# Key and query stacks of an attention unit loaded in pieces of 96, 12, 48 and 6 partitions instead of 54

## The chip, the core and the metric

The kernel runs on one core of a Trainium2 chip. The time is the device time of one execution in microseconds (us); the kernel before has a median of 1902.3 us over three runs (1902.12, 1902.3, 1907.2). A core has engines that run their own instruction streams: TensorE (PE; its weight loads are shown as PEld), VectorE (DVE), ScalarE (ACT), GpSimd (POOL) and SyncE (SP). SP does no arithmetic here: it issues DMAs, in order, and waits in its queue for what a DMA needs. 16 DMA engines move the data.

## What is computed

One layer on x (2048 tokens, width 576): an adaptive layer norm whose shifts and gates come from silu(c) @ w_mod, attention with a memory over four segments of 512 tokens (32 heads of width 18), then a second adaptive layer norm and a SwiGLU feed-forward of width 4608. All in float32.

```python
for s in range(N):                       # N = 4 segments of L = 512 tokens
    logits = einsum("bhqd,bhkd->bhqk", qs, ks) * scale + mask
    p = softmax(logits)
    a_dot = einsum("bhqk,bhkd->bhqd", p, vs)
    num = einsum("bhld,bhde->bhle", phi(qs), M)
    den = einsum("bhld,bhd->bhl", phi(qs), z)[..., None] + 1e-6
    outs.append(g * (num / den) + (1 - g) * a_dot)
    M, z = M + einsum("bhld,bhle->bhde", phi(ks), vs), z + phi(ks).sum(2)
x = x + ga * (concat(outs) @ wo)
h = layernorm(x) * (1 + cb) + sb
return x + gb * ((silu(h @ w_gate) * (h @ w_up)) @ w_down)
```

## The kernel before

Float32 products are made from parts of fewer bits: a tile is split into a high part and a low part (`fh`, `fl`; `hh`, `hl`), and TensorE multiplies the parts that matter. For the attention logits this is done by stacking: a head has 18 features, and its stack has 3 × 18 = 54 rows, the high part of a key or query beside the low part of the other.

The program has four stages.

The projections (to about 256 us). For each segment `proj` (L456) makes nine tiles of keys and queries, copies each out of PSUM on ScalarE (L466), splits it (GpSimd L80, VectorE L81), and stores the parts to DRAM tensors `kD[s]` and `qD[s]` of shape (576, 3, 512): one feature, three parts, 512 tokens, so that the 54 rows of a head lie together (L471 to L478); later segments' queries are stored once more, whole, as `qF` (L480). `vproj` makes the values in eight groups a segment (copied out at L498) and `mem` (L447) the memory. `trans_in` normalizes and transposes the next segment's input (PE L236, evacuated by ScalarE at L243). The order of instructions in this stage is made by an automatic scheduler, which also places the first three stack loads and part of the first units' work: the generator `early` (L255) loads the stacks of units 0 and 1 and later of unit 2.

The loop over units (256 to 616 us). A unit is four heads of one segment, so there are 32; there the order is written out by hand (a manual schedule, with a table `PAT` of events for each of eleven steps of a unit). A unit's work is spread over three passes of the loop. First its stack is loaded by `load_stack` (L160). Then `p1_step` (L174) multiplies queries by keys (PE L184) only to get each query's largest logit on VectorE (`mx`, L189). GpSimd turns it into a high and a low part of its negative (`mc`, L194 to L197), TensorE transposes them (`pmt`, L203), ScalarE copies them (`mr`, L207), and `put_m` (L169) stores them by two small DMAs (L172) into rows 108 and 109 of the query stack. So the second product (PE L599, 110 rows) subtracts the largest logit by itself, and ScalarE's exponential (`Pt`, L606) needs no bias. Last come GpSimd's mask (L610) and the product with the values (PE `av`, L623). Other events of the loop prepare the output weights (`woraw`, loaded at L908), the output projection (`pw`, L733), its residual sum (`xr`, `xD`, L738 and L740), queries for the memory (`qf`, L776), values (`vq`, L668) and the layer norm's output (L938, L958).

The stack tiles are in SBUF: `kst` has 128 partitions x 2 x 512 floats and `qst` 128 x 4 x 512. Four buffers of each rotate (`NB = 4`). A unit's four heads are two pairs; pair a uses slot a of `kst`, and in the pair the head e has its 54 rows on partitions 54e to 54e + 53. A query's rows go to slot e + 2a and the rest of that slot is zero, so that one product over 108 rows gives one head.

SP issues all of these loads in order. Completion of its DMAs is counted on eight semaphores that are used in turn, so each DMA also waits for the one eight before it in this queue.

Behind the loop come a tail of the output projection (616 to 660 us) and the feed-forward (660 us to the end), which loads no stacks.

Of the kernel before, what the change touches and what calls it, by code (L numbers as in the profile page):

```python
# [68 lines left out]
def f32(ap):  # L69
    return ap.bitcast(F32)  # L70
# [3 lines left out]
def block(ctx: ExitStack, tc: tile.TileContext, x, wqk, wv, wo, beta, wgu, wd, c, w_mod, out):  # L74
    nc = tc.nc
# [43 lines left out]
    qst, kst = {}, {}  # L119
# [20 lines left out]
    qD = [dr.tile([D, 3, L], F32, tag=f"qD{s}", name=f"qD{s}") for s in range(NSEG)]  # L140
    kD = [dr.tile([D, 3, L], F32, tag=f"kD{s}", name=f"kD{s}") for s in range(NSEG)]
# [17 lines left out]

    def load_stack(u, b):  # L160
        s, q = units[u]
        for e in range(2):
            v = [d[s].rearrange("f z t -> (f z) t").rearrange("(Q a e r) t -> Q e r a t", Q=8, a=2, e=2)[q, e]
                 for d in (kD, qD)]
            r = slice(54 * e, 54 * e + 54)
            nc.sync.dma_start(f32(kst[b][r]), v[0])
            nc.sync.dma_start(f32(qst[b][r, e:4:2, :]), v[1])

    def put_m(u, b):  # L169
        mr = mrow.pop(u)  # L170
# [75 lines left out]
    with ExitStack() as p1:  # L246
# [8 lines left out]
        def early():  # L255
            for u in range(2):
                load_stack(u, u)
            for u in range(NE):
                yield from p1_unit(u, u, ps, "m", 1, pb, 2)
            load_stack(2, 2)  # L260
# [64 lines left out]
        with ExitStack() as p0:  # L325
# [27 lines left out]
            for p in (1, 0):  # L353
                for k in range(6):
                    for h in range(2):
                        r = 64 * (1 - p) + 32 * h
# [6 lines left out]
            for p in (1, 0):  # L363
                r = 64 * (1 - p) + 32
# [93 lines left out]
        def proj(s, t):  # L458
            hh, hl, hr = hT[s]
            pp = ps.tile([P, L], F32, tag="p", name="pp", bufs=3)  # L460
            mm14(pp, lambda k: wqkh[:, t, k, :], lambda k: wqkl[:, t, k, :], lambda k: hh[k],
                 lambda k: hl[k], lambda: hr, True)
            f = pb.tile([P, L], F32, tag="pf", name="pf")
            fh = pb.tile([P, L], F32R, tag="fh", name="fh")
            fl = pb.tile([P, L], F32R, tag="fl", name="fl")
            nc.scalar.copy(f, pp)  # L466
            split(fh, fl, f)
            k0, k1 = 128 * t, min(128 * t + 128, D)
            if k0 < D:
                n = k1 - k0  # L470
                nc.sync.dma_start(kD[s][k0:k1, 0:2, :], f32(fh[:n]).unsqueeze(1).to_broadcast([n, 2, L]))  # L471
                nc.sync.dma_start(kD[s][k0:k1, 2, :], f32(fl[:n]))
            q0, q1 = max(128 * t - D, 0), 128 * t + 128 - D
            if q1 > 0:
                n = q1 - q0
                r = P - n
                nc.sync.dma_start(qD[s][q0:q1, 0:3:2, :], f32(fh[r:]).unsqueeze(1).to_broadcast([n, 2, L]))
                nc.sync.dma_start(qD[s][q0:q1, 1, :], f32(fl[r:]))  # L478
                if s > 0:
                    nc.sync.dma_start(qF[s][q0:q1, :], f[r:])  # L480
            return f
# [34 lines left out]
        for s in range(NSEG):  # L516
# [12 lines left out]
            for t in QKORD:  # L529
# [4 lines left out]
                f = proj(s, t)  # L534
# [44 lines left out]
    def load_unit(u):  # L579
        if u < NU:  # L580
            load_stack(u, u % NB)
# [733 lines left out]
    def plain(t, p, c):  # L1315
        b, h, c = c // 4, c // 2 % 2, c % 2
        pd = ps.tile([P, 2, L], F32, tag="dn", name="pd", bufs=2)
        for i in range(2):
            tk = slice(128 * (2 * c + i), 128 * (2 * c + i) + 128)
            k = 0  # L1320
            for f in range(2):
                ah, al = AP[p % 2, (f, b)]
                dh, dl = DP[p % 2, (f, h)]
                for a, w in ((ah, dh), (ah, dl), (al, dh)):
                    nc.tensor.matmul(pd[:, i, :288], lhsT=a[:, tk], rhs=w, start=(k == 0), stop=(k == 5))  # L1325
                    k += 1
        d = x11[1] if t and b and h else acc[2 + h + 2 * b]
        o = d[:, 2 * c:2 * c + 2]
        nc.vector.tensor_tensor(o, o, pd[:, :, :288], op=ALU.add)  # L1329
        if p == NPR - 1:  # L1330
            if t:
                store(t, b, h, d, c)
            elif c == 1:
                return lambda: store(t, b, h, d)
# [9 lines left out]
    with tc.manual_schedule():  # L1344
# [6 lines left out]
        for u in range(NU + 1):  # L1351
            s, q = divmod(u, 8)
# [101 lines left out]
        for t in range(2):  # L1454
            for p in range(NPR):
# [16 lines left out]
                for k in range(14):  # L1472
                    z, m = ZM[k]
# [67 lines left out]
                    if prev is not None and is_plain(*prev):  # L1541
# [3 lines left out]
                        if CH0[t][k]:  # L1545
                            f = plain(*prev, chunk)
# [97 lines left out]
```

## Time and profile before

| | us |
|---|---|
| median of three runs | 1902.3 |
| the profiled execution: its own time | 1904.4 |
| its span, first to last instruction | 1902.7 |
| PE busy | 1851.9 (97%) |
| DVE busy | 1500.7 (79%) |
| ACT busy | 935.8 (49%) |
| POOL busy | 583.2 (31%) |
| stack loads: first issue to last | 72.6 to 570.8 |
| granted TensorE clock, mean over the span | 0.995 |

A row of the timeline has the start, the length, the engine, the line of the kernel and the operation with output and input tiles; in brackets stands how long the engine was idle before it and what ended that idle time. A row of waits says for whom an engine waited, how long in all, how often, and the longest. A row of a windows view gives, for a stretch of time, its length, each engine's busy time with the number of instructions, the granted clock of TensorE (1.00 is full speed), the mean busy share of the 16 DMA engines and GB/s. DMA issues on SP take SP's time; the transfer itself runs later on the DMA engines.

### The profile page before, as it was taken

To read this page: it belongs to the slowest core of one execution; us is meant where nothing else is said; L and a number is where in the kernel's file an instruction comes from. 1 tells how busy PE (TensorE), PEld (TensorE's weight loads), DVE (VectorE), ACT (ScalarE), POOL (GpSimd) and SP (SyncE) were. 2 spreads that over 40 slices of the span, in tenths; PEclk is the share of its full clock that TensorE was granted. 3 is DMA by queue.
4 is the path that set the end of the run, shared out by engine and by line. 5 is a ranking of instruction groups with operands and counts; after the bars stand their busy time and mean duration, and the time that the engine had idled before them with its cause. 6 is when DMAs were issued, how large, how long until landed. Compare 5 with 4: busy or idle time off the path is not lost.

```text
span 1902.7 us, 30767 instructions
## 1 busy us (share of the span) xinstructions
PE 1851.9 (97%) x10927; PEld 1573.5 (83%) x10927; DVE 1500.7 (79%) x3277; ACT 935.8 (49%) x2060; POOL 583.2 (31%) x789
## 2 busy tenths in 40 slices
PE   7999989999999899999999999999999999999999
PEld 4888866777776788888888888888888888888888
DVE  6566357878886688898897988876888888888887
ACT  1222267767777444445455454444544454454542
POOL 5212235555556544545444535400000000000000
PEclk9999999999999899999999999999999999999999
DMA  6767555445754764454454554478333233333331
GB/s 197 257 223 250 200 184 149 122 143 160 200 167 126 274 209 160 157 194 156 156 191 154 166 178 140 138 259 260 102 121 104 82 119 102 124 102 100 108 107 60
DMA packets 179425, 304.32 MB, mean 160 GB/s; under 512 B 26152, under 2 KB 107688, under 8 KB 177352
## 3 DMA queue, kind: packets, MB, share of 16 engines
q1 hardware_dynamic: 150696, 245.29, 41.0%
q10 hardware_dynamic: 28576, 57.07, 8.5%
q8 instruction: 86, 1.41, 0.3%
q14 instruction: 67, 0.55, 0.1%
HBM read 187.98 MB, written 113.77 MB: 159 GB/s over the span
## 4 chain that ended last, share of the span: by engine, by line
PE 85%; DMA 4%; DVE 3%; ACT 3%; POOL 2%; issue 1%; SPq 1%; ACTq 0%; DVEq 0%; POOLq 0%
PE A L1204 23%; PE pd L1325 13%; PE C L1204 12%; PE pd L1308 9%; PE B L1204 6%; PE pp L100 5%; PE av L623 3%; PE pv L100 3%; PE s L599 3%; PE s L184 3%; PE pw L733 1%; ACT Pt L606 1%; DMA qs<-mr 1%; PE pm L450 1%; PE pr L358 1%
## 5 line engine op out<-in xcount | busy, mean ns | idle before, releaser
L1204 PE MATMUL A<-y,wh 128*128 128x512 f32 x1152 | 404.7, 392 | 1.8 <-ACT B L1250 1.0
L189 DVE CUSTOM_DVE_ANT_0 junk<-s,tri 128x256 bf16<-128x256 f32 (+3 forms) x512 | 222.9, 485 | 76.0 <-PE s L184 57.6
L1169 DVE TENSOR_TENSOR wl<-O,wh 128x256 fp32r<-128x256 f32 x504 | 262.3, 525 | 3.5 <-ACT wh L1168 3.1
L1204 PEld LDWEIGHTS A<-y,wh 128*128 128x128 f32 x1152 | 216.7, 188 | 43.4 <-ACT B L1250 2.4
L1204 PE MATMUL A<-y,wl 128*128 128x512 f32 x576 | 224.8, 390 | 0.0
L606 ACT ACTIVATE Pt<-s 128x512 f32<-128x512 f32 (+1 forms) x352 | 188.0, 559 | 58.8 <-PE av L623 25.4
L1159 POOL TENSOR_TENSOR O<-O 128x384 f32<-128x384 f32 x140 | 157.9, 1140 | 163.3 <-DMA O<-in_wgu_dram 81.6
L1204 PE MATMUL C<-y,wh 128*128 128x512 f32 x576 | 203.7, 394 | 4.1 <-DMA y<-yD 2.9
L1313 DVE TENSOR_TENSOR acc<-acc,pd 128x576 f32<-128x576 f32 x216 | 162.3, 751 | 54.9 <-PE pd L1308 50.1
L1168 ACT CAST wh<-O 128x256 fp32r<-128x256 f32 x504 | 197.0, 405 | 3.0 <-DVE wr L1154 1.6
L1325 PE MATMUL pd<-dh,ah 128*128 128x288 f32 x640 | 189.8, 297 | 0.1
L1325 PE MATMUL pd<-dh,al 128*128 128x288 f32 x640 | 188.2, 294 | 0.0
L1325 PE MATMUL pd<-dl,ah 128*128 128x288 f32 x640 | 188.2, 294 | 0.0
L1329 DVE TENSOR_TENSOR acc<-acc,pd 128x576 f32<-128x576 f32 x156 | 116.7, 749 | 80.3 <-PE pd L1325 79.9
L599 PE MATMUL s<-qs,ks 110*128 110x512 f32 (+2 forms) x384 | 149.6, 405 | 14.0 <-ACT Pt L606 9.5
L1268 ACT CAST ah<-sg 128x512 fp32r<-128x512 f32 x192 | 119.3, 621 | 86.1 <-DVE sg L1228 80.6
L184 PE MATMUL s<-ks,qs 108*128 108x256 f32 (+3 forms) x512 | 142.2, 330 | 1.4 <-DVE mx L189 1.3
L1269 DVE TENSOR_TENSOR al<-sg,ah 128x512 fp32r<-128x512 f32 x192 | 134.6, 701 | 8.0 <-ACT ah L1268 7.7
L1308 PE MATMUL pd<-dh,ah 128*128 128x288 f32 x448 | 132.9, 297 | 0.0
L1308 PE MATMUL pd<-dl,ah 128*128 128x288 f32 x448 | 131.9, 294 | 0.0
L1308 PE MATMUL pd<-dh,al 128*128 128x288 f32 x448 | 131.2, 293 | 0.0
L1204 PEld LDWEIGHTS C<-y,wh 128*128 128x128 f32 x576 | 108.2, 188 | 24.4 <-DMA y<-yD 3.3
(364 smaller groups left out, 4408.1 us busy)
## 6 DMA issues: line engine op xcount, KB each, us to landing
O<-in_wgu_dram SPq DMA_DIRECT2D x36, 768.0 KB
oD<-O ACTq DMA_DIRECT2D x36, 512.0 KB
O<-oD SPq DMA_DIRECT2D x36, 512.0 KB
ks<-kD SPq DMA_DIRECT2D x64, 216.0 KB
qs<-qD SPq DMA_DIRECT2D x64, 216.0 KB
O<-in_wgu_dram SPq DMA_DIRECT2D x36, 384.0 KB
rD<-wr ACTq DMA_DIRECT2D x36, 336.0 KB
wr<-rD SPq DMA_DIRECT2D x35, 336.0 KB
```

The lines of the kernel that those rows point to most:

```text
L100: nc.tensor.matmul(ps, lhsT=a, rhs=b, start=(k == 0), stop=(k == 13))
L184: nc.tensor.matmul(bank[:, n * (h - h0):n * (h - h0) + n], lhsT=qst[b][0:108, h, 128 * i:128 * i + 128], rhs=kst[b][0:108, h // 2, 0:n], s ...
L189: nc.vector.tensor_tensor_reduce(junk[:, :n], bank[:, n * (h - h0):n * (h - h0) + n], tri[:, L - n:], 1.0, -3e38, op0=ALU.add, op1=ALU.max ...
L599: nc.tensor.matmul(bank[:, n * (g - h):n * (g - h + w)].rearrange("p (a b) -> p a b", a=w), lhsT=kst[u % NB][0:110, g // 2, 128 * j:128 * ...
L606: nc.scalar.activation(pt[:, h:h + per, :n], bank[:, :n * per].rearrange("p (a b) -> p a b", a=per), AF.Exp, scale=SCALE)
L1159: eng.tensor_tensor(o[:, d], o[:, a], o[:, b], op=op)
L1168: nc.scalar.copy(wh, o)
L1169: later.append(lambda: nc.vector.tensor_tensor(wl, o, f32(wh), op=ALU.subtract))
L1204: nc.tensor.matmul(bank, lhsT=a, rhs=b, start=(first and n == 0), stop=(n == 6), skip_group_check=not first)
L1308: nc.tensor.matmul(pd[:, i, :288], lhsT=a[:, tk], rhs=w, start=(k == 0), stop=(k == 2))
L1313: nc.vector.tensor_tensor(o, o, pd[:, :, :288], op=ALU.add)
L1325: nc.tensor.matmul(pd[:, i, :288], lhsT=a[:, tk], rhs=w, start=(k == 0), stop=(k == 5))
```

## The change

Only `load_stack` changes. Before, it issues four DMAs of 54 partitions x 2 x 512 floats (216 KB each), for each e one of keys and one of queries. After, keys are loaded whole, since both heads of a pair go to the same slot of `kst`: partitions 0 to 95, then 96 to 107. Queries must go to different slots for the two heads, so they stay apart: 48 rows of each head and then the last 6 of each. That makes six DMAs (384, 48, 192, 192, 24 and 24 KB), with the same bytes to the same places, 864 KB for a unit. The source rows are 2 KB each in both.

```diff
     def load_stack(u, b):
         s, q = units[u]
-        for e in range(2):
-            v = [d[s].rearrange("f z t -> (f z) t").rearrange("(Q a e r) t -> Q e r a t", Q=8, a=2, e=2)[q, e]
-                 for d in (kD, qD)]
-            r = slice(54 * e, 54 * e + 54)
-            nc.sync.dma_start(f32(kst[b][r]), v[0])
-            nc.sync.dma_start(f32(qst[b][r, e:4:2, :]), v[1])
+        k, v = [d[s].rearrange("f z t -> (f z) t").rearrange("(Q a r) t -> Q r a t", Q=8, a=2)[q] for d in (kD, qD)]
+        for r0, r1 in ((0, 96), (96, 108)):
+            nc.sync.dma_start(f32(kst[b][r0:r1]), k[r0:r1])
+        for r0, r1 in ((0, 48), (54, 102), (48, 54), (102, 108)):
+            nc.sync.dma_start(f32(qst[b][r0:r1, r0 // 54:4:2, :]), v[r0:r1])
```

Over the 32 units the stack loads go from 128 DMAs to 192, all on SP's queue. In the loop over units and behind it, the order of all other instructions on each engine is the same in both kernels. In the projections, where a scheduler decides, the same instructions stand in another order on PE, DVE, ACT and POOL in places, up to the end of segment 2's projections. The changed kernel's lines behind this function have numbers lower by one.

## The prediction

> **What bounds the kernel now.** I read the page's first lines, then the busy time of each engine by stage, then what TensorE waited for in the stage where the stacks are loaded, and last the DMA queue's own timeline around those waits.
>
> ```profile
> span 1902.7 us, 30767 instructions
> PE 1851.9 (97%) x10927; PEld 1573.5 (83%) x10927; DVE 1500.7 (79%) x3277; ACT 935.8 (49%) x2060; POOL 583.2 (31%) x789
> ...
> 0.00:70.00 70.00, 55.85 (x251) 39.51 (x252) 48.39 (x90) 15.22 (x27) 36.89 (x63) 0.98 0.73 222
> 70.00:256.00 186.00, 183.11 (x1099) 159.86 (x1098) 89.82 (x209) 46.45 (x88) 39.11 (x65) 1.00 0.67 228
> 256.00:616.00 360.00, 341.71 (x2592) 252.05 (x2592) 280.62 (x1176) 271.93 (x556) 201.03 (x382) 0.99 0.52 151
> 616.00:660.00 44.00, 35.32 (x197) 31.53 (x196) 28.02 (x48) 18.48 (x40) 20.67 (x20) 0.88 0.78 271
> 660.00:1903.00 1243.00, 1235.93 (x6795) 1090.57 (x6793) 1053.89 (x1754) 583.73 (x1352) 285.46 (x260) 1.00 0.45 145
> ```
>
> Each stage row gives its length, the busy time of PE, weight load, DVE, ACT and POOL, the granted clock, the DMA share and GB/s. PE sets the time. The stack loads touch two stages only: the projections (70 to 256 us, 186 − 183.11 = 2.9 us of PE idle time) and the loop over the 32 units (256 to 616 us, 360 − 341.71 = 18.3 us idle). So whatever better loads can bring is at most 21.2 us, plus time lost to a low clock. In the loop this is what PE waited for (total, times, longest), and where the stack loads and the two small rows `qs<-mr` stand among all issues:
>
> ```profile
> PE s L599 <- ACT Pt L606: 9.5, 15, 1.7
> PE s L599 <- DMA qs<-mr: 3.4, 5, 1.1
> ...
> L167 SPq DMA_DIRECT2D qs<-qD x64: 265/344/887, 73.5 to 570.8; - x64
> L172 SPq DMA_DIRECT2D qs<-mr x64: 508/580/1217, 115.0 to 601.0; - x64
> ...
>   DMA ks<-kD: 0.2, 1
> ...
> ks<-kD SPq DMA_DIRECT2D x64, 216.0 KB
> ```
>
> PE hardly waits for the stacks themselves (`ks<-kD`: 0.2 us in all); it waits five times for `qs<-mr`, two DMAs of 8 KB that are issued on SP right after a stack load. The five places, and SP's queue ahead of the second:
>
> ```profile
> 285.31 0.77 PE L599 MATMUL s<-qs,ks 110*128 110x512 f32 x1 [1.07 <-DMA qs<-mr]
> ...
> 308.63 0.47 PE L599 MATMUL s<-qs,ks 110*128 110x512 f32 x1 [1.03 <-DMA qs<-mr]
> ...
> 381.64 0.47 PE L599 MATMUL s<-qs,ks 110*128 110x512 f32 x1 [0.61 <-DMA qs<-mr]
> ...
> 475.62 0.46 PE L599 MATMUL s<-qs,ks 110*128 110x512 f32 x1 [0.21 <-DMA qs<-mr]
> ...
> 570.57 0.47 PE L599 MATMUL s<-qs,ks 110*128 110x512 f32 x1 [0.48 <-DMA qs<-mr]
> ```
>
> ```profile
> 299.10 0.33 SPq L908 DMA_DIRECT2D woraw<-in_wo_dram  x1
> 299.54 0.29 SPq L166 DMA_DIRECT2D ks<-kD  x1
> 299.88 0.35 SPq L167 DMA_DIRECT2D qs<-qD  x1
> 300.58 0.27 SPq L166 DMA_DIRECT2D ks<-kD  x1
> 300.91 0.33 SPq L167 DMA_DIRECT2D qs<-qD  x1
> 302.03 1.16 SPq L172 DMA_DIRECT2D qs<-mr  x2
> ...
> 302.60 5.90 DMA qs<-mr
> ```
>
> The last line is from the chain of waits: the second small DMA took 5.90 us to land. The load was issued only 1 to 2.5 us ahead of it, and the 8 KB sit behind its 864 KB.
>
> **The change part by part.** *The transfers.* How wide a load spreads shows in the DMA share (last column but one) and rate:
>
> ```profile
> 265.00:269.50 4.50, 4.42 (x43) 2.40 (x34) 2.43 (x9) 3.10 (x6) 2.49 (x6) 1.00 0.57 176
> ...
> 418.50:419.00 0.50, 0.50 (x10) 0.13 (x4) 0.00 (x0) 0.00 (x0) 0.34 (x2) 1.00 1.05 382
> 419.50:424.50 5.00, 5.00 (x47) 4.22 (x40) 3.73 (x12) 3.05 (x7) 1.48 (x6) 1.00 0.59 175
> 437.00:438.00 1.00, 1.00 (x8) 0.95 (x7) 0.93 (x5) 0.98 (x3) 0.24 (x1) 1.00 0.08 17
> ```
>
> While a stack alone is landing the share stays at 0.57 to 0.59, about 9 engines of 16 (0.56), at 175 GB/s; where other transfers run, all 16 give 382 GB/s. So 54 partitions use 9 engines. 54 partitions of 2 rows of 2 KB (512 floats) are 108 packets, 12 on each of 9 engines, 48 for the four DMAs; 864 KB at 175 GB/s is 5.1 us, or 0.105 us a packet.
>
> My reading of the division is that a DMA uses the largest number of engines up to 16 that divides its partitions: 54 gives 9, 96 and 48 give 16, 12 gives 12, 6 gives 6. The busiest engine then holds 12 packets (96 partitions) + 2 (12) + 6 + 6 (48 twice) + 2 + 2 (6 twice) = 30, and the load lands in 30 × 0.105 = 3.2 us, 1.9 us sooner. Bounds: nothing gained (still 9 engines) and 864 KB at 382 GB/s = 2.3 us, 2.8 us sooner. I take 1.9, from the division that explains 0.57.
>
> The Trainium skill, page "DMA: Bandwidth & Descriptors", section "Why a DMA increments its semaphore by 16 and not by 1", states this division for the slowest dimension of both sides; the trace agrees for 54 (0.57), and shows no load of 96, 12, 48 or 6 partitions. The same page, section "Rules for kernel authors", speaks against the change: small transfers should be coalesced, since below 64 KB one pays mostly overhead, and splitting one transfer into disjoint partition ranges isn't worth while; of the six new pieces three lie below that mark.
>
> *The five waits.* If small DMAs behind the load land 1.9 us sooner, waits of 1.07, 1.03, 0.61, 0.21 and 0.48 us (3.4 in all) all go; by the lower bound none does. The first lies at half clock (the clock is the number ahead of the DMA share):
>
> ```profile
> 282.00:283.00 1.00, 0.28 (x1) 0.29 (x2) 1.00 (x8) 1.00 (x3) 0.74 (x1) 0.89 0.49 158
> 283.00:284.00 1.00, 1.00 (x6) 1.00 (x5) 0.82 (x3) 1.00 (x3) 0.74 (x2) 0.50 0.11 22
> ...
> 285.00:289.00 4.00, 3.69 (x19) 1.09 (x23) 0.21 (x2) 0.60 (x1) 2.27 (x5) 0.50 0.73 221
> 289.00:290.00 1.00, 1.00 (x20) 0.51 (x12) 0.00 (x0) 0.00 (x0) 0.00 (x0) 0.70 0.58 170
> ```
>
> The clock falls near 282.9, ahead of that wait, after a wait for ACT. If the low stretch keeps its end, work moved 1.07 us forward inside it is worth half, 0.5; if it ends as much earlier, 1.07. I take 0.8: with the others 3.1 us. What PE meets next is ACT's exponentials (`Pt`, 9.5 us over the loop), which start as much earlier because PE feeds them.
>
> *Two more issues per unit.* From 299.54 to 299.88 and 300.58 to 300.91 an issue occupies SP for 0.34 us, so two are 0.7 us a unit (32 units, 22 us). They lie in SP's own waiting, not on PE's path:
>
> ```profile
> SPq L172 <- ACT mr L207: 52.4, 15, 5.9
> SPq L172 <- ACT Pt L606: 43.1, 12, 7.0
> ```
>
> Before 27 of the 32 small pairs SP stands waiting (95.5 us, 3.5 each) for ACT's copy of `mr`. In the tight place above, the last issue ends at 301.24 and the pair starts at 302.03: 0.79 us, still over 0.7. Queued behind the loads are also the loads of `vq`, `yh` and `yq`, none of which PE waited for in this loop. Cost taken: 0; if the cover fails everywhere, 22 us.
>
> *The projections.* There the instruction order comes from the scheduler, and the changed kernel issues a different order between about 70 and 215 us on PE, ACT, DVE and POOL, with the same instructions; later only SP's loads differ. PE's longest waits there (total, times, longest):
>
> ```profile
> PE s L184 <- DVE mx L189: 1.0, 1, 1.0
> PE pmt L203 <- POOL mc L197: 0.9, 1, 0.9
> PE pp L100 <- DVE hr L81: 0.5, 2, 0.3
> ```
>
> The moved `pmt` may lose the second. What stands to be lost is at the end of segment 2:
>
> ```profile
> 185.78 0.59 ACT L466 COPY pf<-pp 128x512 f32<-128x512 f32 x1 [3.25 <-DMA qF<-pf]
> ...
> 196.98 0.78 ACT L243 ACTIVATE hf<-pt,colv 128x512 f32<-128x512 f32 x1
> ```
>
> In the new order the first evacuation of the next segment's transposes (L243, 0.78 us) stands ahead of the last three copies of projection tiles (L466), and its transposes come right after the last projection, at 185.2. Three PSUM banks hold those three tiles, so the V groups wait: the third transpose waits for the first evacuation (0.45), the first V group for a copy (0.15), the second perhaps for the next one (0 to 0.6), the last transposes for a later evacuation (0.4). That is 1.0 to 1.6, less the 0.5 us of waits for the split `hr`, around 209 us. Bounds for the whole stage −1.9 to +1.6; taken +0.3.
>
> *Sum.* −3.1 + 0 + 0.3 = −2.8 us: the span 1902.7 becomes 1899.9, its run (1904.4, 1.7 above its span) 1901.6. That profiled run is 2.1 us above the median 1902.3, so against the median I expect **1899.5 us**. Bounds of the terms: loop −3.4 to 0, stage before it −1.9 to +1.6: −5.3 to +1.6.
>
> **The rivals.** *More is gained.* The stretch at half clock goes as well: between 282.9 and 289.6 PE is busy about 5.6 us at half speed, worth 2.8 us, and `pmt`'s 0.93 us goes without a cost at 185 us: −3.4 − 2.8 − 0.9 = −7.1, 1895.2 us. For it: PE is starved by the same late loads. Against it: the clock falls before the wait for `mr`, after one for ACT.
>
> *SP becomes late (the other side).* The six issues reach past the moment at which `mr` is ready, so the small pair starts later and PE waits for `qs<-mr` in units where it now doesn't. It decides where less than 0.7 us lies between the last load's issue and the pair. If that holds in the 15 units whose pair follows ACT's copy directly, it costs up to 15 × 0.7 = 10.5 us, less the 3.1 gained: +7.4, 1909.7 us. For it: the margin of 0.79 in the tight place, and longest issues of 887 ns. Against it: waits of 3.5 us on average at just this point. By the skill's rule on small transfers named above the pieces would bring overhead of this kind; the trace shows that the 8 KB pair alone occupies the engines at 0.08 for 1 us, which is little.
>
> *The spread doesn't change.* The pieces run on as few engines as before, or the six queue up so that they end no sooner: 0 in the loop, +0.3 before it, 1902.6 us. Against it: the share of 0.57, which fits 9 of 16 so well.
>
> **How the numbers follow.** 0.3% of 1902.3 us, about what a measurement of this kernel can tell from no change, is 5.7 us. Forecast 0.50 (0.44 within 0.3%, 0.06 faster), more gained 0.24 (faster), SP late 0.18 (0.15 slower, 0.03 within), no wider spread 0.08 (within). Faster 0.30, same 0.55, slower 0.15. The forecast's own range is 1897 to 1904 (its bounds). Reaching to the centre of the larger gain with 2 us beyond it, and to the lower part of the late SP, the range is 1893 to 1907; half of the SP case and a part of the larger gain stay outside.
>
> **What would show it.** Right: after a load the DMA share rises from 0.57 towards 0.9 for about 3 us; the row "PE s L599 <- DMA qs<-mr" shrinks from 3.4 us to under 0.5; two more issues of about 0.34 us lie ahead of `qs<-mr`, and SP's waits at L172 shrink by up to 0.7 us each; stages from 660 us on keep their length; the projections end within 2 us of 256. Wrong: a loop as long as before (the transfers were hidden or not wider), a longer wait for `qs<-mr` (SP), the clock at 283 to 289 back at 1.00 (more gained), or a projection stage with PE idle for over 5 us, which my hand count at 185 us doesn't hold.

## The result, and the profile after

The changed kernel is faster by a third of a per cent. Its median is 1898.38 us over 22 runs (1894.64 to 1902.62), against 1903.68 us for the kernel before over 22 runs (1899.04 to 1916.07); the ratio is 0.9967 with a 95% interval of 0.9957 to 0.9977, that is 4 to 8 us less. Of the prediction, 1899.5 us lies 1.1 us above the measured median; against the median of the runs shown then (1902.3) it stood for 2.8 us gained, and 5.3 were gained between the new medians. The gain lies at the edge of what the prediction took as the least that a measurement of this kernel can tell (0.3%, 5.7 us).

First the page of the changed kernel, and its stages (columns as before):

```profile
span 1895.8 us, 30849 instructions
PE 1849.9 (98%) x10927; PEld 1572.9 (83%) x10927; DVE 1499.9 (79%) x3277; ACT 935.1 (49%) x2060; POOL 586.3 (31%) x789
...
DMA packets 180577, 304.32 MB, mean 161 GB/s; under 512 B 27304, under 2 KB 108840, under 8 KB 178504
```

```profile
70.00:256.00 186.00, 183.76 (x1102) 160.46 (x1100) 93.10 (x218) 47.09 (x90) 41.48 (x67) 1.00 0.69 233
256.00:616.00 360.00, 345.22 (x2636) 256.57 (x2635) 283.29 (x1180) 273.61 (x560) 204.78 (x386) 1.00 0.58 156
```

The profiled span is 6.9 us shorter than before. The fixed windows show PE fuller in the loop over units, but since all work has moved ahead, marks in the work say more. The second products (`qs`, `ks`) ran from 255.3 to 613.2 us before:

```profile
L598 PE MATMUL s<-qs,ks x384: 274/399/735, 253.9 to 606.5; 110*128 110x512 f32 x96, 110*128 110x384 f32 x64, 110*128 110x256 f32 x32
```

The loop starts 1.4 us sooner and takes 352.6 us instead of 357.9, so 5.3 us of the 6.9 were gained in it and 1.4 ahead of it; behind it the two runs differ by 0.2 (marks that a view gives to 0.1 us leave about 0.1 us open in such differences). What PE waited for in the loop, now:

```profile
PE s L598 <- ACT Pt L605: 9.3, 15, 1.7
PE av L622 <- DVE ol L716: 1.6, 4, 0.6
PE pto L705 <- POOL o L660: 1.4, 3, 0.7
```

The row for `qs<-mr` (3.4 us, 5 times) is gone, and the row for the exponentials is about as long as before (9.3 against 9.5): the time gained did not turn into a new wait. At the first of the five places the timeline of PE shows what was 285.31 with 1.07 us of waiting, and a product `av` of 4.1 us at half clock behind it:

```profile
282.82 0.50 PE L598 MATMUL s<-qs,ks 110*128 110x256 f32 x2 [1.36 <-ACT Pt L605]
283.16 0.56 PE L183 MATMUL s<-ks,qs 108*128 108x128 f32 x4
283.88 0.50 PE L598 MATMUL s<-qs,ks 110*128 110x512 f32 x1 [0.16 <-ACT Pt L605]
284.31 2.36 PE L622 MATMUL av<-Pt,vq 128*32 128x512 f32 x32
```

The hole of 1.36 us ahead of it is still there (1.35 before), so it wasn't the hole alone that brought the clock down here. SP's timeline shows the price, two more issues ahead of the small rows, here at the first place and then at the second, the tight one of the prediction:

```profile
276.05 0.36 SPq L907 DMA_DIRECT2D woraw<-in_wo_dram  x1
276.50 0.84 SPq L164 DMA_DIRECT2D ks<-kD  x2
277.40 1.53 SPq L166 DMA_DIRECT2D qs<-qD  x4
279.02 1.15 SPq L171 DMA_DIRECT2D qs<-mr  x2
...
296.08 1.92 SPq L164 DMA_DIRECT2D ks<-kD  x2
298.05 1.52 SPq L166 DMA_DIRECT2D qs<-qD  x4
299.67 1.15 SPq L171 DMA_DIRECT2D qs<-mr  x2
```

At the first place the loads' last issue ends at 278.93, with ScalarE's copy ready at 278.90. At the second the copy is ready before SP is:

```profile
298.62 0.24 ACT L206 COPY mr<-pmt 32x128 f32<-32x128 f32 x1
```

It ends at 298.86, and the rows are issued 0.81 us later; before, they were issued 0.03 us after it. So SP has become late there. It cost nothing, because the rows land behind the load in any case: in the trace's records of the DMAs' semaphores, both before and after, the second row of this unit lands 0.4 us after the load's last piece. Over the 29 loads of the loop that follow the scheduler's part, these records put the last piece 7.9 us after the load's first issue before and 6.6 us in the change (medians), so the load lands 1.3 us sooner.

The transfer itself, in a stretch in which one stack is landing alone, is first shown for the kernel before and then for the changed one:

```profile
431.00:433.50 2.50, 2.50 (x33) 1.56 (x26) 0.80 (x2) 1.56 (x3) 1.28 (x6) 1.00 0.59 166
```

```profile
425.75:428.25 2.50, 2.50 (x33) 1.53 (x26) 0.79 (x4) 1.59 (x3) 1.24 (x6) 1.00 1.04 274
```

The share rises from 0.59 to full (a packet's whole time is counted in the stretch in which it starts, so that a short stretch can come out above 1), but the rate from 166 to 274 GB/s only. In steps of half a microsecond the share falls off about 6 us after the load's first issue before, and about 5 after the change.

### The profile page after: what moved, and what is told of

It is laid out like the page before. It is cut to its first block, busy times and chain, and to the rows that moved or that the text cites. A ratio compares the mean times of both kernels' runs of the same rounds, so it can differ in the third digit from the quotient of the medians.

```text
span 1895.8 us, 30849 instructions
## 1 busy us (share of the span) xinstructions
PE 1849.9 (98%) x10927; PEld 1572.9 (83%) x10927; DVE 1499.9 (79%) x3277; ACT 935.1 (49%) x2060; POOL 586.3 (31%) x789
## 2 busy tenths in 40 slices
DMA packets 180577, 304.32 MB, mean 161 GB/s; under 512 B 27304, under 2 KB 108840, under 8 KB 178504
## 4 chain that ended last, share of the span: by engine, by line
PE 84%; ACT 4%; DVE 4%; DMA 3%; POOL 3%; issue 2%; SPq 1%; ACTq 0%; POOLq 0%; DVEq 0%
PE A L1203 23%; PE pd L1324 12%; PE C L1203 11%; PE pd L1307 9%; PE B L1203 6%; PE pp L100 5%; PE av L622 3%; PE pv L100 3%; PE s L183 3%; PE s L598 3%; DMA y<-yD 2%; ACT Pt L605 2%; PE pw L732 1%; PE pm L449 1%; DVE junk L188 1%
## 5 line engine op out<-in xcount | busy, mean ns | idle before, releaser
L1168 DVE TENSOR_TENSOR wl<-O,wh 128x256 fp32r<-128x256 f32 x504 | 266.4, 533 | 4.3 <-ACT wh L1167 3.5
```

What stands on the lines that cost most here:

```text
L1168: later.append(lambda: nc.vector.tensor_tensor(wl, o, f32(wh), op=ALU.subtract))
```

## The experiments

All kernels but e10 differ from the changed kernel in `load_stack` only, and e12 not at all; "in the loop" means units 3 to 31, whose loads lie behind the scheduler's part. Each profile gives one execution, and stretches at half clock come and go in the first three units. So beside the time I compare the stretch from unit 3's product `av` to the last second product: it was 316.6 us before (296.63 to 613.2) and 313.0 in the change (293.49 to 606.5). The ratios are each against the kernel before, run again beside the experiment.

| kernel | load in the loop | stretch, us | whole loop, us | PE waits for `qs<-mr`, us | ratio of times, 95% interval |
|---|---|---|---|---|---|
| before | 54 x 4 | 316.6 | 357.9 | 3.4 | 1 |
| the change | 96, 12, 48, 48, 6, 6 | 313.0 | 352.6 | 0 | 0.9967 (0.9957 to 0.9977) |
| e1 | as the change | 312.9 | 352.5 | 0.3 | 0.9977 (0.9966 to 0.9988) |
| e2 | 54 x 4 | 316.3 | 359.0 | 2.4 | 1.0002 (0.9991 to 1.0013) |
| e3 | 54, 54, 27 x 4 | 314.2 | 357.4 | 2.3 | 0.998 (0.9968 to 0.9993) |
| e4 | 48, 48, 12, 32, 16, 32, 16, 6, 6 | 313.0 | 353.6 | 0 | 0.9967 (0.9956 to 0.9977) |
| e8 | 54 x 4, keys first | 316.1 | 358.8 | 2.4 | 0.999 (0.9981 to 1.0) |
| e9 | 27 x 8 | 314.2 | 356.4 | 1.8 | 0.9982 (0.997 to 0.9994) |
| e6 | 54, 54, 48, 48, 6, 6 | 313.8 | 356.0 | 0.6 | 0.9975 (0.9964 to 0.9986) |
| e7 | 108, 48, 48, 6, 6 | 312.8 | 351.2 | 0.5 | 0.9966 (0.9953 to 0.9979) |
| e11 | as e7, for all units | 313.2 | 355.7 | 0 | 0.9978 (0.9968 to 0.9987) |
| e12, the change again | as the change | 313.1 | 353.7 | 0 | 0.9959 (0.9946 to 0.9972) |
| e10 | 54 x 4, `mr` on ScalarE's queue | 337.8 | 382.4 | 1.7 | 1.0122 (1.0101 to 1.0143) |

**Which part: e1 and e2.** e1 loads the first three stacks as before, so that the projections keep the old instruction order; e2 is the reverse.

```diff
+        if u < 3:        # e2: u >= 3
+            for e in range(2):
+                r = slice(54 * e, 54 * e + 54)
+                nc.sync.dma_start(f32(kst[b][r]), k[r])
+                nc.sync.dma_start(f32(qst[b][r, e:4:2, :]), v[r])
+            return
```

> The stacks of units 0 to 2 are loaded in pieces of 54 as before (so the projections have the old instruction order), all others in the new pieces. Width theory (a load on 16 engines lands sooner and lets the small mr rows behind it land sooner): the loop starts at 255.3 us as before, the row for qs<-mr (3.4 us, 5 times) is gone, and the last unit's product comes 3.4 us sooner, or about 5.3 if the stretch at half clock around 283 to 289 us goes too. Rival (the gain comes from the other order of the projections, which shifts the loop): the five waits stay and the time is within 1 us of before.

> The new pieces for the stacks of units 0 to 2 alone, so that the projections have the new instruction order; the loop loads 54 as before. Width theory: the loop starts 1.4 us sooner, at 253.9, and then has its five waits for qs<-mr again, 3.4 us in all, so that the time is 1.4 us below before; the half clock may lie at 262 to 266 us as in the changed kernel or at 283 to 289 as before. Rival (the order of the projections is what removes them): the five waits are gone, 5 to 7 us below before.

The loop loads alone bring the loop's gain (352.5 us) and a time 0.23% below before. The new order of the projections alone leaves three of the waits, shown in e2's row:

```profile
PE s L604 <- DMA qs<-mr: 2.4, 3, 1.3
```

Its time is that of before within a tenth of a per cent: the gain ahead of the loop is at most small beside the runs' spread. Its loop starts at 251.1 us, not at 253.9, and e1's at 256.3, not at 255.3. Most of that arises before 70 us (the first projections' matmul on `hr` ran at 35.9 us in e2 and 38.6 before), where no stack is loaded, and e1 has a lower clock at 40 to 60 us; so the loop's start in one profile is no measure of this change to a microsecond. From that matmul to the last value product it is steadier: 216.6 us before, and 215.1, 215.1 and 215.2 in the change, e2 and e4. It too has to be read with the clock: in e3, e7 and e12, which have the same order, it is 216.7 to 216.8 us, with 3.4 us at half clock near 40 us, and in e1, which has the old order and such a stretch as well, 218.2. Where the clock is the same, the new order is 1.5 us shorter.

**Width or number: e3, e8, e9.** e3 has six DMAs as the change has, but all of a size that divides by 9 and by no larger number up to 16. e8 only changes the order (keys, keys, queries, queries), e9 has eight pieces of 27. The cuts here and below leave out the condition that keeps the first three units as in the change.

```diff
-        for r0, r1 in ((0, 96), (96, 108)):
+        for r0, r1 in ((0, 54), (54, 108)):                                # e9: four of 27
             nc.sync.dma_start(f32(kst[b][r0:r1]), k[r0:r1])
-        for r0, r1 in ((0, 48), (54, 102), (48, 54), (102, 108)):
+        for r0, r1 in ((0, 27), (54, 81), (27, 54), (81, 108)):            # e8: (0, 54), (54, 108)
             nc.sync.dma_start(f32(qst[b][r0:r1, r0 // 54:4:2, :]), v[r0:r1])
```

> In the loop six DMAs as in the change, but of 54, 54, 27, 27, 27 and 27 partitions, all of which divide by 9 and by nothing larger up to 16; the first three stacks as in the change. Width theory: DMA share after a load stays at 0.57, the waits for qs<-mr are back with 3 to 4.5 us (the load is issued 0.7 us later), the loop is as long as before or up to 1 us longer, total -1.4 to 0 us against before. Rival (more and smaller pieces let the small DMA through, whatever their width): the waits are gone as in the change, total -5 to -7 us.

> In the loop four DMAs of 54 partitions as before, but both of the keys first and then both of the queries (before they alternate). The measure: from the product av of unit 3 to the last second product it took 316.6 us before, 313.0 in the change, 314.2 with six narrow pieces. If the order of the pieces explains what the six narrow ones gained: about 314, waits for qs<-mr under 1.5 us from 296 us on. If it was the smaller size, or chance: 316 to 317 and the waits of before.

> In the loop eight DMAs of 27 partitions (9 engines each, the width of before, 48 packets an engine). If smaller pieces land sooner at the same width: the same stretch takes 314.2 us or less and the load's DMA share ends at or before 5.6 us after its first issue (6.2 before, 5.65 with six narrow pieces). If size does not matter and only width does: 316 us, and up to 1 us more since two more issues stand ahead of qs<-mr. Share near 0.57 in both cases.

e3's DMA share while a stack lands alone, and its waits in the loop:

```profile
430.80:433.30 2.50, 2.50 (x33) 1.57 (x26) 0.80 (x2) 1.53 (x3) 1.32 (x6) 1.00 0.59 199
```

```profile
PE s L598 <- ACT Pt L605: 8.9, 13, 1.7
PE s L598 <- DMA qs<-mr: 2.3, 4, 1.4
```

The share stays at 0.59 and the loop is about as long as before, which is what width alone would say. But behind unit 3 e3 and e9 take 314.2 us, 2.4 less than before, about 2 less than e2 and e8 (316.3 and 316.1) and only 1.2 more than the change. Their time is 0.2% below before (for e3 3.8 us, where 0 to 1.4 were expected), and by time alone they can't be told from e1 (0.9977). So smaller pieces at the same width help too, and the order doesn't. This was not expected.

It is not that every load of 27s lands sooner. At the second of the five places PE waits for the row at 308.63 before and at 308.67 in e3; the load had its first issue at 299.54 and 300.41. From there to the product are 9.1 us before and 8.3 in e3, although its two more issues stand between. At the first place it is the other way round: PE waits 1.4 us in e3 and e9, and 0.6 to 0.7 in e2 and e8. Over the loop's 29 loads the last piece lands 7.5 and 7.6 us after the first issue (medians of e3 and e9), against 7.7 and 7.5 in e2 and e8. What the packets' records show is that one of 2 KB takes 100 ns on average in e3 and e9, and 105 to 112 in the loads of 54 (before, e2, e8), taken over the 18 to 20 loads beside which no other packets of 2 KB ran. Why it does stayed open.

**How many engines a piece takes: e6 and e7, and the packets of all.** e6 has the new queries and the old keys, e7 the new queries and the keys in one DMA of 108 partitions.

```diff
-        for r0, r1 in ((0, 96), (96, 108)):
+        for r0, r1 in ((0, 108),):                  # e6: (0, 54), (54, 108)
```

> In the loop keys in 54 and 54, queries in 48, 48, 6 and 6. By width alone the busiest engine holds 12 + 12 + 6 + 6 + 2 + 2 = 40 packets instead of 48 (30 in the change): about half of the change's effect, 314 to 315 us for the stretch from unit 3's product to the last second product, one to three waits for qs<-mr left. If only getting rid of small differences counts, 313.

> In the loop the keys in one DMA of 108 partitions (12 engines by the division, 18 packets each), queries as in the change: five DMAs, 34 packets on the busiest engine against 30. Width theory: share near 0.75 while the keys land, no wait for qs<-mr over 0.3 us, stretch 313 us as in the change; one issue fewer on SP. If 108 goes to fewer engines (9 or 6), the waits return: 315 us or more.

e7's share, in the same stretch of its load:

```profile
425.30:427.80 2.50, 2.50 (x33) 1.52 (x26) 0.79 (x2) 1.47 (x3) 1.36 (x6) 1.00 0.93 247
```

The half-changed load lies between (313.8 us, waits of 0.2 us at the longest), as counted, though nearer to the change than halfway. e7 does as well as the change with one DMA fewer. One wait of 0.5 us is left, against 0.3 expected. The loads land 6.9 and 6.8 us after their first issue (medians of e6 and e7), between 7.9 before and 6.6 in the change. Its share of 0.93 is for a stretch in which the queries had been issued too, so it isn't the 0.75 that was expected for the keys alone.

The division itself can be counted. The line of packets for the kernel before is

```profile
DMA packets 179425, 304.32 MB, mean 160 GB/s; under 512 B 26152, under 2 KB 107688, under 8 KB 177352
```

and the change has 27304 − 26152 = 1152 more packets under 512 B, with the same bytes. If each DMA ends with one small packet on every engine that it uses, a load had 4 x 9 = 36 and now has 16 + 12 + 16 + 16 + 6 + 6 = 72; 36 more for 32 units is 1152. The same count for the others (29 units in the loop, the first three as in the change):

| kernel | small packets a load in the loop, by the division | so above before | measured above before |
|---|---|---|---|
| e1 | 72 (first three 36) | 29 x 36 = 1044 | 1044 |
| e3 | 9 x 6 = 54 | 29 x 18 + 108 = 630 | 630 |
| e4 | 16 x 2 + 12 + 16 x 4 + 6 x 2 = 120 | 29 x 84 + 108 = 2544 | 2544 |
| e6 | 9 x 2 + 16 x 2 + 6 x 2 = 62 | 29 x 26 + 108 = 862 | 862 |
| e7 | 12 + 16 x 2 + 6 x 2 = 56 | 29 x 20 + 108 = 688 | 688 |
| e9 | 9 x 8 = 72 | 29 x 36 + 108 = 1152 | 1152 |

The sums alone could come out of other divisions, but the records of each DMA's semaphore agree piece by piece: in the loop they hold 10 increments for every piece of 54 or 27, 13 for 108 or 12, 16 for 96, 48, 32 and 16, and 7 for 6, which is one for each engine by the division, and one more where there are fewer than 16. So 54 and 27 partitions take 9 engines, 108 and 12 take 12, 96, 48, 32 and 16 take 16, and 6 take 6. The Trainium skill's page "DMA: Bandwidth & Descriptors" (section "Why a DMA increments its semaphore by 16 and not by 1") states just this division, and this case agrees in every size.

**What the issues cost: e4.** The same width, three more issues a unit than the change.

```diff
-        for r0, r1 in ((0, 96), (96, 108)):
+        for r0, r1 in ((0, 48), (48, 96), (96, 108)):
...
-        for r0, r1 in ((0, 48), (54, 102), (48, 54), (102, 108)):
+        for r0, r1 in ((0, 32), (32, 48), (54, 86), (86, 102), (48, 54), (102, 108)):
```

> In the loop nine DMAs of 48, 48, 12, 32, 16, 32, 16, 6 and 6 partitions: the engines that each byte goes to are as wide as in the change, with three more issues (about 1.05 us of SP a unit more than the change, 1.8 us more than before). Width theory with SP covered: waits for qs<-mr under 1 us in all, total within 1.5 us of the change. Rival (SP is near its limit): the mr pair starts later in the tight units (margin 0.79 us before), waits for qs<-mr of over 3 us in all, and the gain of the loop is lost; in the worst case 32 x 1.05 = 34 us more.

No wait for `qs<-mr` comes back, and the stretch is 313.0 us as in the change. The issues eat SP's waiting instead. SP's waits in the loop, first in the change, then in e4:

```profile
SPq L171 <- ACT Pt L605: 32.4, 15, 5.6
SPq L171 <- ACT mr L206: 30.5, 13, 5.0
```

```profile
SPq L171 <- ACT Pt L605: 18.5, 12, 4.3
SPq L171 <- ACT mr L206: 15.1, 11, 3.6
```

From 95.5 us before they shrink to 62.9 and 33.6; by the number of issues added (64 and 151) that is 0.51 and 0.41 us an issue, more than the 0.34 that one takes by itself. Nine DMAs leave 33.6 us, about 1 us a unit on average, but not in every unit: in e4 the rows of units 3 and 5 are issued 2.2 us after their copy is ready, and PE still doesn't wait for them.

**The queue of the small rows: e10.** Here the loop loads 54 x 4 as before, and the two DMAs of `mr` go to ScalarE's queue.

```diff
-            nc.sync.dma_start(f32(qst[b][108 + a:109 + a]).rearrange("p a t -> p (a t)"), mr[16 * a:16 * a + 16])
+            (nc.scalar if u > 2 else nc.sync).dma_start(f32(qst[b][108 + a:109 + a]).rearrange("p a t -> p (a t)"), mr[16 * a:16 * a + 16])
```

> In the loop the stacks are loaded as before (four DMAs of 54), but the two small DMAs of mr are issued on ScalarE's queue, so that they no longer stand behind the load in SP's queue; the first three stacks as in the change. If the gain is only that the small rows stop queueing behind the load: no wait for qs<-mr over 0.3 us, stretch from unit 3's product to the last second product 313 to 314 us although the stacks land as late as before. If PE needs the stacks themselves sooner: 316 us. If the two issues on ScalarE cost (it works 272 of 360 us in the loop): up to 0.7 us a unit more waits for Pt, over 320 us.

It fails as a test of the queueing, since the issues cost far more than they could bring:

```profile
304.54 1.15 ACTq L177 DMA_DIRECT2D qs<-mr  x2
```

```profile
PE s L604 <- ACT Pt L611: 28.0, 42, 1.8
...
PE s L604 <- DMA qs<-mr: 1.7, 1, 1.7
```

1.15 us of ScalarE a unit delays the exponentials; PE waits 28.0 us for them instead of 9.5, and the loop is 24.5 us longer. ScalarE is busy for 272 of 360 us in the loop before and yet has no 1.15 us to spare at this point, while SP's 1.15 us are free. Nor do the rows get past the load on that queue: the second row of this pair, issued while a load is landing, lands 6.25 us after the first one's issue, 1.0 us behind the load's last piece, and wherever a load is landing in e10's loop, the second row lands behind it. So what rows that got past the load would bring isn't decided by it.

**A better split: e11, beside e12.** e11 loads the keys of all units in one DMA of 108; e12 is the change once more on the same chip.

> Keys in one DMA of 108 partitions (12 engines), queries as in the change, for all 32 units: five DMAs. The loop as with 108 in the loop alone (351 to 353 us); the projections get another instruction order than in the change, from which I expect between 1.5 us gained and 1.5 us lost against before. Total 3 to 8 us below before, within 2 us of the change.

> The change itself once more, for comparison with the other two on the same chip: ratio 0.9957 to 0.9977 as measured first, no wait for qs<-mr, stretch of 313.0 us. Whether a stretch at half clock lies at unit 0 (av of 3.5 us instead of 2.36) may differ from the first profile.

e11's loop has no wait for `qs<-mr` and 313.2 us behind unit 3, but its time is 0.22% below before and e12's 0.41%. Its loop takes 355.7 us where 351 to 353 were expected, and its median is 3.0 us above e12's, not within 2. Its projections have yet another instruction order, and in its profile two stretches at half clock (10.2 us in all) lie in the first three units. No version that ran beats the change by more than the runs can tell.

## Why the prediction was right, and what was mis-sized

*What bounds the kernel, and where a load can matter.* Right: PE sets the time, and the gain came from PE's waits for the small rows behind a load, not from the stacks themselves. All five waits are gone in the change, and with loads of 54 in the loop three of them are back (e2, e8; 2.4 us of 3.4).

*The transfer.* The division of engines was right to the packet. The time was off: 30 packets of 0.105 us gave 3.2 us, 1.9 sooner, and over the loop's 29 loads the last piece lands 1.3 us sooner. The step that was mis-sized is the fixed price of a packet. With all engines at work a packet of 2 KB takes longer: 133 ns on average in the change against 112 before. An estimate from these, 48 x 0.112 less 30 x 0.133, is 1.4 us. Landing 1.3 us sooner was still enough for waits of up to 1.07 us. And width isn't all: e3 and e9 show that smaller pieces of the old width, at 100 ns a packet, give about 2 us behind unit 3. What only the wide loads show is the rest, 1.2 us, and the first place: e3 and e9 still wait 1.4 us there.

*The five waits.* Taken: 3.1 us for the loop. Measured: 5.3 and, in e12, 4.2. Behind unit 3 it was 3.6 us where the four waits summed to 2.3: each place gave 0.1 to 0.3 us more than its wait in the row. At unit 18's first product (452.45 before), where the profile of before puts a wait of 0.30 us down to `Pt`, 0.5 us were gained as well. By the semaphores' records the second row landed there at 452.31, as far ahead of its product as at the other places (0.13 to 0.14 us), so this looks like a sixth wait for the row. But e2 and e8, with loads of 54, gain the same there, since their load landed 0.7 and 1.0 us sooner than the one of before. So about 3.1 us are left for the new pieces.

The larger part of the misjudged size is the clock. I took 0.8 us for the first wait and left the stretch at half clock in place, with its removal as a rival worth 2.8. In the change it is gone from 283 to 289 us; another one appeared around unit 0 (its `av` takes 3.47 us), which the profile of before didn't have. Over the profiles this varies: the time from the first second product to unit 3's `av` is 41.3, 42.6, 43.2, 42.7, 42.2 us with narrow loads (before, e2, e3, e8, e9) and 39.6, 40.7, 39.6, 40.6, 38.4 and 42.5 with wide ones (the change, e12, e1, e4, e7, e11): 42.4 against 40.2 on average. The granted clock over this stretch is 0.92 before and 0.96 in the change:

```profile
255.34:296.63 41.29, 35.87 (x227) 22.47 (x225) 30.00 (x126) 31.70 (x64) 20.22 (x31) 0.92 0.48 148
...
253.87:293.49 39.62, 35.07 (x226) 21.92 (x224) 30.47 (x128) 31.99 (x64) 20.57 (x32) 0.96 0.55 153
```

Length times what the clock lacks of 1.00 is an estimate of the time lost to it: 4.4 us on average with narrow loads, 2.6 with wide ones. So of the 2.2 us between them, where 0.8 were counted, about 1.9 are the clock. The half clock that sets in between 280 and 287 us lasts 6.8 us with narrow loads (3.4 in e9), and 0 or 3.4 us, three profiles each, with wide ones. So the rival that saw this stretch go was right in part. That sooner rows shorten it fits most of these profiles but isn't shown as the cause: in the kernel before the clock falls ahead of the wait, and e6, which has no wait there, has 6.8 us too. Around unit 0, whose stack is loaded ahead of the loop, such stretches come and go as well.

*Two more issues per unit.* The cost of 0 was right, the reason only in part. The prediction set 0.7 us of issues against 0.79 us of cover in the tight place; there the loads' issues took 3.49 us instead of 1.70, since the two of the keys alone took 1.92 us (0.84 at the first place), and the rows were issued 0.81 us late. On average the waits at the rows shrank by 1.0 us a unit, not by up to 0.7. That it cost nothing comes from the rows' place behind the load, whose landing sets when they land. So the rival's premise, a late SP, came true in the tight units, and its price didn't, even with nine DMAs (e4). Nor did the pieces under 64 KB bring an overhead that PE felt.

*The projections.* Taken +0.3, and the profile says −1.5 between the same two marks (216.6 to 215.1 us). Of the losses that I counted two are there (0.43 and 0.25 us, at 184.6 and 202.2, against 0.45 and 0.4), and the two of the V groups aren't:

```profile
184.63 0.66 PE L235 MATMUL pt<-ident,x 128*128 128x128 f32 x4 [0.43 <-ACT hf L242]
...
202.16 0.63 PE L235 MATMUL pt<-ident,x 128*64 128x128 f32 x4 [0.25 <-ACT hf L242]
```

The gains were larger: the wait of 0.95 us for `mx` at 102 us is gone, which I had credited in the bound alone, and `pmt` waits 0.38 us instead of 0.93. In e2's time, though, this 1.5 us doesn't stand out.

*The sum.* By profile the change gives 5.3 in the loop and 1.5 ahead of it, where 2.8 net was forecast; the mechanism of the forecast held, and the terms were too small: about 1.8 us in the projections, 0.9 to 1.4 at the first place with its clock, and 0.8 at the places behind unit 3 (1.3 with unit 18). A range of 1893 to 1907 us covers all of that, so that the time fell inside it says less than the waits that went.

## What to carry to other kernels

Look at the DMA share while one transfer lands alone: a plateau well under 1 (0.59 here) can mean that its partition count uses only part of the engines, and one cut at a multiple of 16, with a small remainder of its own, filled them here. Keys in one DMA of 108 partitions, on 12 engines, did as well (e7). Count what the extra issues take from the issuing queue's waits before worrying about them, but only on a queue that has such waits, or where what it issues late would have had to wait anyway. And in a kernel bound by PE, look for small late DMAs behind a large one: the row that PE waits for may be the small one.

## What the hardware showed that was not expected

With all 16 engines at work on one stack load the share went from 0.59 to 1.04 and the rate from 166 only to 274 GB/s; a packet of 2 KB took 133 ns on average instead of 112. In pieces of 27 partitions it took 100 ns, on 9 engines as with 54, for a reason that stayed open. Two rows of 8 KB landed in 2.4 us where no load was landing, and at the first two of the five places 0.3 to 0.4 us behind the load's last piece, before and after; on ScalarE's queue they didn't get past it either. And with more DMAs on a queue whose completions are counted on eight semaphores, SP began to wait for the load ahead at the small rows (`SPq L171 <- DMA ks<-kD`, 4.8 us in four places, against 1.2 in one before), which here cost PE nothing.
